# A column per chunk for the output scales, k's features one slot behind q's, and v's parts counted against their due slot

## The chip, the core and the metric

The kernel runs on one NeuronCore of a Trainium2 chip. Five engines work side by side, each on its own queue of instructions in a fixed order: TensorE (PE in the profile, its weight loads PEld), VectorE (DVE), ScalarE (ACT), GpSimd (POOL) and SyncE (SP), which here only starts DMAs. An engine whose next instruction has to wait stands, with everything queued behind it. The metric is the device time of one execution in microseconds.

## The reference

Random-feature attention for 8 batches, 8 heads, 576 positions, 64 dimensions and 128 features, and a bilinear feed-forward block behind it:

```python
q_s, k_s = (q * scale, k * scale)
def phi(x):
    proj = np.einsum('bhsd,md->bhsm', x, omega)
    sq = np.sum(x * x, axis=-1, keepdims=True) / 2.0
    h = proj - sq
    h = h - np.max(h, axis=-1, keepdims=True)
    return np.exp(h) / np.sqrt(m)
q_p, k_p = (phi(q_s), phi(k_s))
kv = np.einsum('bhsm,bhsd->bhmd', k_p, v)
z = np.sum(k_p, axis=2)
num = np.einsum('bhsm,bhmd->bhsd', q_p, kv)
den = np.einsum('bhsm,bhm->bhs', q_p, z)[..., None] + 1e-06
x = num / den                       # to 4608 tokens x 512
out = ((x @ w1) * (x @ w2)) @ w3 @ w_out
```

The kernel subtracts no square: it falls away with the maximum that is subtracted behind it. It multiplies w3 and w_out into one matrix first.

## The kernel before

The 4608 positions are 36 chunks of 128. A batch is 576 positions, so it covers four and a half chunks, and its sum over k needs five of them. Every float32 operand of a matmul is split into two float16 parts, `hi` and `lo`, after a scaling by a power of two, and each product is three matmuls (`PASSES`). The split is the helper at L137: ACT writes `hi`, DVE subtracts to get `lo` (L144; qhl, khl, vhl, xhl in the profile).

A chunk of q or k goes through these stages. `load` (L211) brings it into one of two raw buffers. `norm` (L223) takes its square sum on ACT (L158, junk_q and junk_k) and `scale` (L229) turns this into a scale by way of a small matmul (norm_q_k). `split_raw` (L238) splits it, after which the chunk two further on is loaded. `features` (L250) projects it on PE into two PSUM banks (L265, qpj and kpj), takes the maximum on DVE (L275, nm), subtracts it (L288, qe and ke) and takes the exponential on ACT (L289). `in_parts` (L292) splits the features: for q DVE casts (L130, eq) and POOL subtracts (L298); for k ACT casts (L132, ek) and POOL subtracts.

q's features are turned by a DMA and multiplied by a batch's key-value sum in `q_attend` (L370; PE's nu at L381, then gd, gr and xs on DVE, then mx, the maximum over xs). `kv_batch` (L339) makes that sum (PE's kvp at L346, kv on ACT and DVE). The projections, nu and kvp all take their PSUM from one pool of two buffers (`banks`, L110): each waits until the reader of the buffer two before it is through, which is qe, ke, xs or kv. `x_turn` (L406) scales and splits the attention's output (xhl), turns it by a DMA into xT, and keeps the power of two in pt.

The feed-forward block works on pairs of chunks: `gate` (L604; PE's ab at L617, asb on ACT at L626 and on DVE at L627, then two POOL instructions into the arena) and `project_out` (L637; osc at L639, PE's o at L643, ACT's scaled copy o at L647, and the DMA to the output). osc is one column, pt times pt times the weights' scale kap, out of four rotating buffers (`small`, L116): a new one waits until the ACT copy that read the buffer's last content is done.

v goes through a list of parts per batch (`v_batch`): five square sums on ACT, a scale, five splits. `v_unit` takes one part from the list's head.

What is written when is set by a table of slots. A step i begins at slot `begin[i]`, three slots a step, and treats q's chunk i and k's chunk i + 5. In every slot one unit is taken from the queue of gates and output projections, then the functions that were put at the slot run in the order of their rank, then one part of v's list runs. A scheduler that keeps the program's data dependencies lays the instructions into the engines' queues; it moves an instruction ahead of others where it takes its operands to be ready. So osc, which the program writes with its output projection, stands on DVE several slots ahead of it.

Of the kernel before, what the change touches and what calls it, by code (L numbers as in the profile page):

```python
# [9 lines left out]
F32 = mybir.dt.float32  # L10
# [9 lines left out]
P = 128  # L20
# [30 lines left out]
EAGER = 40  # L51
EARLY = 6
KV_LAG = 5
RAW64_BUFS = 3
O_BUFS = 2
RAW_BUFS = 2
# [10 lines left out]
def tile_favor_attention_then_bilinear_ffn(  # L67
# [20 lines left out]
    NCH = qT.shape[0]  # L88
# [14 lines left out]
    const = ctx.enter_context(tc.tile_pool(name="const", bufs=1))  # L103
# [9 lines left out]
    def bank_m(name):  # L113
        return ps_m.tile([P, 512], F32, tag="pm", name=name)

    def small(name, n=1, rows=P, dt=F32, bufs=4):  # L116
        return sm.tile([rows, n], dt, tag=f"s_{name}", name=name, bufs=bufs)
# [16 lines left out]
    def pick(kinds, i):  # L134
        return kinds[min(i, len(kinds) - 1)]
# [68 lines left out]
    def chunks_of(b):  # L204

        lo, hi = b * S, (b + 1) * S
        return [(c, max(lo - c * P, 0), min(hi - c * P, P)) for c in range(lo // P, -(-hi // P))]
# [10 lines left out]
    for i in range(4):  # L218
        t = const.tile([P, 3], F32, name=f"sums_{i}")
# [3 lines left out]
    def norm(keys, n):  # L223
        am = sums[n % len(sums)]
        for i, k in enumerate(keys):
            square_sum(am[:, i : i + 1], raws[k], f"{k[0]}{k[1]}", QK_PRE)
        return am
# [10 lines left out]
    def split_raw(c, name):  # L238

        raw = raws.pop((name, c))  # L240
        s, es = scales.pop((name, c))
        hl = at.tile([P, 2, NP, P], F16, tag="hl", name=f"{name}hl_{c}", bufs=2)
        split(pick(KS if name == "k" else QS, c), hl[:, 0], hl[:, 1], raw, s)
        hls[name, c] = hl, es
# [5 lines left out]
    def features(c, name):  # L250


        hl, es = hls.pop((name, c))
        pg = banks(f"{name}pj_{c}").rearrange("p g (i m) -> p g i m", m=M)
        pj = pg.rearrange("p g i m -> p (g i) m")

        def project(first=None):
            for i in range(NP):
                if first is not None:
                    for g in range(2):  # L260
                        nc.tensor.matmul(pg[:, g, i], ident, first(g * NP + i), start=True, stop=False)
                for n, (x, y) in enumerate(PASSES):
                    for g in range(2):
                        d = slice(g * D, (g + 1) * D)
                        nc.tensor.matmul(  # L265
                            pg[:, g, i],
                            hl[d, x, i],
                            om[d, y],
                            start=first is None and n == 0,
                            stop=n == len(PASSES) - 1,  # L270
                        )

        project()
        nm = small("nm", H)
        nc.vector.tensor_reduce(nm, pj, AX.X, ALU.max, negate=True)  # L275
        e = at.tile([P, H, M], F32, tag="e", name=f"{name}e_{c}", bufs=2)
        kind = pick(DK if name == "k" else DQ, c)
        if kind == "2":

            project(lambda h: nm[:, h : h + 1].broadcast_to([P, M]))  # L280
            nc.scalar.activation(e, pj, AF.Exp, scale=es, bias=ln_e)
        elif kind == "1":

            nc.vector.tensor_scalar(nm, nm, es, 15 * math.log(2.0), ALU.mult, ALU.add)
            for h in range(H):
                nc.scalar.activation(e[:, h], pj[:, h], AF.Exp, scale=es, bias=nm[:, h : h + 1])
        else:
            nc.vector.tensor_tensor(e, pj, nm.unsqueeze(2).broadcast_to([P, H, M]), ALU.add)  # L288
            nc.scalar.activation(e, e, AF.Exp, scale=es, bias=ln_e)  # L289
        return e  # L290

    def in_parts(t, e, hi, lo):  # L292

        if hi == "p":
            nc.gpsimd.tensor_scalar(t[:, 0], e, 1.0, 1.0, ALU.mult, ALU.mult)
        else:
            copy(hi == "d", t[:, 0], e)
        (nc.vector if lo == "d" else nc.gpsimd).tensor_tensor(t[:, 1], e, t[:, 0], ALU.subtract)  # L298
# [3 lines left out]
    def k_chunk(c):  # L302
        e = features(c, "k")
        ek[c] = at.tile([P, 2, H, M], F16, tag="ek", name=f"ek_{c}", bufs=EK_BUFS)
        in_parts(ek[c], e, pick(EH, c), pick(EL, c))
# [136 lines left out]
    arena = const.tile([P, ARENA, 512], F32, name="arena")  # L442
    raw_at = list(range(0, 4 * RAW64_BUFS, 4))
    mag_at = list(range(4 * RAW64_BUFS, 4 * RAW64_BUFS + 4, 2))
    free = list(range(4 * RAW64_BUFS + 4, ARENA))

# [6 lines left out]
    def used(at):  # L453

        left[at] -= 1
        if not left[at]:
            free.append(at)
# [146 lines left out]
    def gate(c0, n, u):  # L604
# [28 lines left out]
        for k in range(nf):  # L633
            for t in range(n):
                hs[c0 + t, u * nf + k] = h[:, :, k, t * P : (t + 1) * P], place

    def project_out(c):  # L637
        sc = small("osc")
        nc.vector.tensor_scalar(sc, pts[c], pts[c], kap, ALU.mult, ALU.mult)  # L639
        ps = bank_m(f"o_{c}")  # L640
        mm = [(f, a, b) for f in range(NF) for a, b in PASSES]
        for i, (f, a, b) in enumerate(mm):
            nc.tensor.matmul(ps, hs[c, f][0][:, a], W[f][:, b], start=i == 0, stop=i == len(mm) - 1)  # L643
        for f in range(NF):
            used(hs[c, f][1])
        o = mo.tile([P, DO], F32, tag="o", name=f"o_{c}", bufs=O_BUFS)
        nc.scalar.mul(o, ps, sc)  # L647
        nc.sync.dma_start(out[c * P : (c + 1) * P, :], o)
# [3 lines left out]
    B_OF_K = {}  # L652
# [3 lines left out]
    v_work = []  # L656
# [7 lines left out]
    def v_unit():  # L664
        if v_work:
            v_work.pop(0)[1]()
# [26 lines left out]
    for ch in ORDER:  # L693
        n = seen.get(ch, 0)
# [23 lines left out]
    def put(slot, rank, fn):  # L718
        plan.setdefault(slot, []).append((rank, len(plan[slot]) if slot in plan else 0, fn))

    behind_by = []

    def ready(c):
        x_turn(c)
        for c0, m in groups:
            if c0 + m == c + 1:
                units = []
                for u in range(2 * m):
                    need = [(n, u // m) for n in range(2)]
                    units.append((need, lambda c0=c0, m=m, u=u: gate(c0, m, u)))  # L730

                for k, f in enumerate(behind_by):
                    units.insert(2 + 3 * k, f)
                behind_by[:] = [(["k"], lambda c=c: project_out(c)) for c in range(c0, c0 + m)]
                queue.extend(units)
                if c + 1 == NCH:
                    queue.extend(behind_by)

    def step(i):
        at0 = begin[i]  # L740
        kc = i + LEAD
        keys = [(n, c) for n, c in (("q", i), ("k", kc)) if 0 <= c < NCH]
        state = {}

        def norms():
            state["am"] = norm(keys, i)

        def splits():
            for name, c in keys:
                split_raw(c, name)  # L750
                if c + 2 < NCH:
                    load(srcs[name], c + 2, name)

        put(at0 - 3, 3, norms)
        put(at0 - 2, 6, lambda: scale(keys, state["am"]))
        put(at0 - 1, 8, splits)
        if i >= 0:
            put(at0, 1, lambda: q_chunk(i))
            lag = 2 if i < EARLY else 5
            put(at0 + lag, 7 if i < EARLY else 0, lambda: q_attend(i))  # L760
            put(at0 + lag + 1, 0, lambda: ready(i))
        if kc < NCH:
            put(at0, 2, lambda: k_chunk(kc))
        if kc in B_OF_K:

            def kv():

                while v_work and v_work[0][0] <= B_OF_K[kc]:
                    v_unit()
                kv_batch(B_OF_K[kc])  # L770


            put(at0 + (2 if i < 0 else KV_LAG - 1 if i < EARLY else KV_LAG), 5, kv)
        for b in range(B):
            cs = [c for c, _, _ in chunks_of(b)]
            if cs[1] == kc:
                put(at0, 9, lambda b=b: v_batch(b))
            if cs[0] == kc:
                put(at0 + 2, 10, lambda cs=cs: [v_load(c) for c in cs if c not in vraw])
# [7 lines left out]
    for t in range(max(plan) + 1):  # L787
        n = min(PER[t] if t < len(PER) else 1, len(ticks))
        weights(n)
        if not ticks and raw_at:  # L790
            for a, w in [(a, 4) for a in raw_at] + [(a, 2) for a in mag_at]:
                free.extend(range(a, a + w))
            raw_at.clear()
        unit(RESERVE if t > EAGER else 0)
        for _, _, fn in sorted(plan.get(t, []), key=lambda x: x[:2]):
            fn()
        v_unit()
    assert not ticks
    while queue:
        unit()  # L800
# [38 lines left out]
```

## Time and profile before

| | |
|---|---|
| median of 3 runs | 906.85 us (904.66 to 910.05) |
| the profiled execution | 904.25 us |
| its span, from the first to the last instruction | 902.5 us |
| PE busy | 790.9 us (88%) |
| DVE busy | 622.6 us (69%) |
| ACT busy | 421.0 us (47%) |
| POOL busy | 322.2 us (36%) |
| granted TensorE clock, mean | 0.951 |

In a row of groups stand line, engine, operation, what is written and read, shapes and count; then busy time in us and the mean of one in ns; then the engine's idle time just ahead of these instructions and what ended it. In a row of time stand the start, the duration, and in brackets the idle time before it with what ended it; a run of equal instructions is one row. A row of windows has the stretch, its length, the busy time of PE, PEld, DVE, ACT and POOL with the number of instructions, the granted clock, the busy share of the DMA engines and GB/s.

### The profile page before, as it was taken

What the parts mean: (1) busy time and instruction counts of PE and PEld (TensorE: products, weight loads), DVE (VectorE), ACT (ScalarE), POOL (GpSimd) and SP (SyncE); (2) the same over time, 40 slices, a digit from 0 to 9 for tenths busy, and PEclk for the clock granted to TensorE, in tenths of its full rate; (3) what the DMA queues carried; (4) which work ended last, traced back from release to release, by engine and by line L of the source; (5) the groups of instructions that cost most, each with busy time, mean ns of one, the idle gap of its engine ahead of it and who ended that gap; (6) DMA issues with size and microseconds to landing.
All of it is one profiled execution on the core that took longest, in us unless ns stands there. A gap on an engine that the chain in (4) does not pass through costs nothing.

```text
span 902.5 us, 20601 instructions
## 1 busy us (share of the span) xinstructions
PE 790.9 (88%) x8614; PEld 586.0 (65%) x8614; DVE 622.6 (69%) x1116; ACT 421.0 (47%) x748; POOL 322.2 (36%) x327
## 2 busy tenths in 40 slices
PE   1964499578996998999999999899899899999998
PEld 0433254476875876767777776777677677677674
DVE  5879877788779887766867777778667774553210
ACT  3677874877436535444354335543454333221111
POOL 0000003223364465443634643455444543323221
PEclk9985699789999999999999999999999999999999
DMA  8535455332345353333434443344332232333000
GB/s 311 191 120 196 140 153 170 111 73 55 88 107 105 84 130 83 83 84 83 116 83 77 95 111 71 72 94 113 85 93 65 60 71 61 82 60 60 24 25 35
DMA packets 142525, 88.43 MB, mean 98 GB/s; under 512 B 116704, under 2 KB 116832, under 8 KB 142432
## 3 DMA queue, kind: packets, MB, share of 16 engines
q1 hardware_dynamic: 134944, 66.15, 31.0%
q10 hardware_dynamic: 7488, 20.97, 6.9%
q8 instruction: 67, 1.10, 0.5%
q14 instruction: 26, 0.21, 0.1%
HBM read 49.35 MB, written 9.44 MB: 65 GB/s over the span
## 4 chain that ended last, share of the span: by engine, by line
PE 42%; DVE 28%; ACT 13%; DMA 9%; issue 6%; POOL 1%; SPq 0%; DVEq 0%; ACTq 0%; POOLq 0%
PE ab L617 20%; PE o L643 11%; DVE nm L275 5%; DVE qhl L144 4%; DMA qraw<-qT 4%; PE wp L557 4%; DVE vhl L144 3%; ACT ke L289 2%; DVE qe L288 2%; DVE ke L288 2%; DMA kraw<-kT 2%; ACT ek L132 2%; PE kvp L346 2%; DVE asb L627 2%; PE nu L381 1%
## 5 line engine op out<-in xcount | busy, mean ns | idle before, releaser
L617 PE MATMUL ab<-xT,w12b 128*128 128x256 f16 (+1 forms) x3840 | 400.3, 265 | 10.8 <-DMA xT<-xhl 8.5
L617 PEld LDWEIGHTS <-w12b 128*128 128x128 f16 x3840 | 345.1, 99 | 54.3 <-issue 8.8
L643 PE MATMUL o<-Wb,arena 128*128 128x512 f16 x864 | 193.4, 379 | 2.1 <-DVE Wb L144 1.6
L643 PEld LDWEIGHTS <-arena 128*128 128x128 f16 x864 | 84.3, 100 | 96.3 <-issue 2.9
L631 POOL TENSOR_SCALAR arena<-asb 128x512 f16<-128x512 f32 x72 | 57.6, 800 | 249.7 <-DVE asb L627 238.3
L298 POOL TENSOR_TENSOR eq<-qe,eq 128x1024 f16<-128x1024 f32 x34 | 73.9, 2174 | 147.9 <-DVE eq L130 111.1
L289 ACT ACTIVATE qe<-qe,ln_e,es 128x1024 f32<-128x1024 f32 x31 | 38.4, 1239 | 138.0 <-DVE qe L288 138.0
L632 POOL TENSOR_TENSOR arena<-asb,arena 128x512 f16<-128x512 f32 x72 | 91.4, 1270 | 5.9
L627 DVE TENSOR_TENSOR asb<-ab,asb 128x512 f32<-128x512 f32 x72 | 49.4, 686 | 52.7 <-PE ab L617 50.6
L144 DVE SCALAR_TENSOR_TENSOR qhl<-qraw,s,qhl 128x512 f16<-128x512 f32 x36 | 63.8, 1773 | 28.7 <-ACT qhl L141 28.7
L158 ACT ACTIVATE junk_q<-qraw 128x512 bf16<-128x512 f32 x36 | 22.7, 630 | 120.4 <-DMA qraw<-qT 120.3
L298 POOL TENSOR_TENSOR ek<-ke,ek 128x1024 f16<-128x1024 f32 x28 | 60.2, 2149 | 41.4 <-DVE ek L130 39.8
L265 PE MATMUL kpj<-om,khl 64*128 64x128 f16 x864 | 36.9, 237 | 43.4 <-DVE xs L396 12.1
L639 DVE TENSOR_SCALAR osc<-pt,kap 128x1 f32<-128x1 f32 x36 | 9.5, 271 | 84.8 <-ACT o L647 84.6
L265 PEld LDWEIGHTS <-khl 64*128 64x128 f16 x864 | 29.4, 103 | 50.2 <-ACT junk_k L158 16.1
L557 PE MATMUL wp<-w12b 128*128 128x512 f32 x128 | 60.2, 623 | 1.2 <-DVE w12b L485 1.2
L626 ACT ACTIVATE asb<-ab 128x512 f32<-128x512 f32 x72 | 41.8, 580 | 24.4 <-PE ab L617 24.4
L381 PEld LDWEIGHTS <-eqT 128*128 128x128 f16 (+1 forms) x960 | 32.5, 102 | 26.0 <-DMA eqT<-eq 15.3
L647 ACT ACTIVATE o<-o,osc 128x512 f32<-128x512 f32 x36 | 24.2, 673 | 52.2 <-PE o L643 52.2
L381 PE MATMUL nu<-kv,eqT 128*128 128x65 f16 (+1 forms) x960 | 34.7, 196 | 15.0 <-DMA eqT<-eq 14.3
L418 DVE SCALAR_TENSOR_TENSOR xhl<-xs,p2r,xhl 128x512 f16<-128x512 f32 x36 | 28.8, 800 | 26.5 <-ACT xhl L417 26.4
L143 POOL TENSOR_SCALAR vhl<-vraw,s 128x512 f16<-128x512 f32 (+1 forms) x35 | 36.3, 1054 | 29.4 <-DVE mx L409 11.7
(124 smaller groups left out, 1071.1 us busy)
## 6 DMA issues: line engine op xcount, KB each, us to landing
kraw<-kT SPq DMA_DIRECT2D x36, 256.0 KB, 3.0
vraw<-v SPq DMA_DIRECT2D x36, 256.0 KB, 3.0
qraw<-qT SPq DMA_DIRECT2D x36, 256.0 KB, 2.7
out<-o SPq DMA_DIRECT2D x36, 256.0 KB, 2.0
arena<-w3T ACTq DMA_DIRECT2D x8, 1024.0 KB, 5.9
arena<-w ACTq DMA_DIRECT2D x8, 1024.0 KB, 5.6
arena<-wo ACTq DMA_DIRECT2D x4, 1024.0 KB, 5.1
eqT<-eq SPq DMA_TRANSPOSE x72, 3.1
```

Source lines behind the costliest of these rows:

```text
L144: nc.vector.scalar_tensor_tensor(lo, src, s, hi, ALU.mult, ALU.subtract)
L265: nc.tensor.matmul(pg[:, g, i], hl[d, x, i], om[d, y], start=first is None and n == 0, stop=n == len(PASSES) - 1,)
L275: nc.vector.tensor_reduce(nm, pj, AX.X, ALU.max, negate=True)
L289: nc.scalar.activation(e, e, AF.Exp, scale=es, bias=ln_e)
L298: (nc.vector if lo == "d" else nc.gpsimd).tensor_tensor(t[:, 1], e, t[:, 0], ALU.subtract)
L381: nc.tensor.matmul(nu[r0:r1, h // 4, h % 4], t[:, x, place(h), r0:r1], kvs[b][:, y, h], start=n == 0, stop=n == 2,)
L557: nc.tensor.matmul(ps, w[:, j, k * P : (k + 1) * P], guest[:, j], start=j == j0, stop=j == HALF - 1,)
L617: nc.tensor.matmul(ps[:, k], w12[m][i][cc][:, a, r * P : (r + 1) * P], x[:, b, cc, off : off + T], start=j == 0, stop=j == len(mm) - 1,)
L627: nc.vector.tensor_tensor(asb, ab[1], asb, ALU.mult)
L631: nc.gpsimd.tensor_scalar(h[:, 0], asb, 1.0, 1.0, ALU.mult, ALU.mult)
L632: nc.gpsimd.tensor_tensor(h[:, 1], asb, h[:, 0], ALU.subtract)
L643: nc.tensor.matmul(ps, hs[c, f][0][:, a], W[f][:, b], start=i == 0, stop=i == len(mm) - 1)
```

## The change

Three edits. The scales of the outputs get one tile with a column for each of the 36 chunks in the place of four rotating buffers. From step 8 on (`K_LATE`), k's features are put one slot later than q's. And in each slot, as many parts of v are taken as keep every batch's parts in time for its slot `due`, at least one.

```diff
+K_LATE = 8
...
+    oscs = const.tile([P, NCH], F32, name="oscs")
+
     def project_out(c):
-        sc = small("osc")
+        sc = oscs[:, c : c + 1]
         nc.vector.tensor_scalar(sc, pts[c], pts[c], kap, ALU.mult, ALU.mult)
...
+    due = {}
...
         if kc < NCH:
-            put(at0, 2, lambda: k_chunk(kc))
+            put(at0 + (i >= K_LATE), 2, lambda: k_chunk(kc))
...
-            put(at0 + (2 if i < 0 else KV_LAG - 1 if i < EARLY else KV_LAG), 5, kv)
+            due[B_OF_K[kc]] = at0 + (2 if i < 0 else KV_LAG - 1 if i < EARLY else KV_LAG)
+            put(due[B_OF_K[kc]], 5, kv)
...
-        v_unit()
+
+        n = max([1] + [-(-(k + 1) // max(due[b] - t, 1)) for k, (b, _) in enumerate(v_work)])
+        for _ in range(n):
+            v_unit()
```

On PE the kpj groups of the last 21 chunks of k (15 to 35, steps 10 to 30) each stand behind the next gate unit instead of right behind qpj; nothing else moves there. DVE's queue in step 15 (a name's number after the tile is the chunk; the last one is a buffer), before:

```order
L275 TENSOR_REDUCE nm_5588<-qpj_15_5563 128x8
L288 TENSOR_TENSOR qe_15_5590<-qpj_15_5563,nm_5588 128x1024
L275 TENSOR_REDUCE nm_5624<-kpj_20_5599 128x8
L288 TENSOR_TENSOR ke_20_5626<-kpj_20_5599,nm_5624 128x1024
L130 CAST eq_15_5593<-qe_15_5590 128x1024
L627 TENSOR_TENSOR asb_10_3_5688<-ab_10_3_1_5663,asb_10_3_5688 128x512
L173 TENSOR_SCALAR norm_q16_k21_5693<-norm_q16_k21_5693 128x3
```

and with the change, from two instructions earlier:

```order
L643 TENSOR_SCALAR oscs_114<-pt_13_5548,kap_111 128x1
L419 SCALAR_TENSOR_TENSOR xhl_13_5551<-xs_13_5472,p2r1_4_5546,xhl_13_5551 128x512
L628 TENSOR_TENSOR asb_10_2_5538<-ab_10_2_1_5513,asb_10_2_5538 128x512
L276 TENSOR_REDUCE nm_5580<-qpj_15_5555 128x8
L289 TENSOR_TENSOR qe_15_5582<-qpj_15_5555,nm_5580 128x1024
L131 CAST eq_15_5585<-qe_15_5582 128x1024
L628 TENSOR_TENSOR asb_10_3_5647<-ab_10_3_1_5622,asb_10_3_5647 128x512
L276 TENSOR_REDUCE nm_5677<-kpj_20_5652 128x8
L174 TENSOR_SCALAR norm_q16_k21_5685<-norm_q16_k21_5685 128x3
L289 TENSOR_TENSOR ke_20_5679<-kpj_20_5652,nm_5677 128x1024
```

k's maximum and subtraction moved behind q's cast and the second gate's asb. The column of the output scale for chunk 13 now stands right behind its pt, ahead of xhl; before, it stood ahead of the next xs.

ACT's queue from k's exponential on, before:

```order
L289 ACTIVATE ke_19_5318<-ke_19_5318,ln_e_82,es_4979 128x1024
L132 CAST ek_19_5321<-ke_19_5318 128x1024
L141 ACTIVATE qhl_15_5484<-qraw_15_4772,s3_4_5391 128x512
L141 ACTIVATE khl_20_5489<-kraw_20_4777,s3_4_5391 128x512
L158 ACTIVATE junk_q17_5922,sums_1_103<-qraw_17_5487 128x512
L647 ACTIVATE o_8_5424<-o_8_5399,osc_5397 128x512
L158 ACTIVATE junk_k22_5924,sums_1_103<-kraw_22_5492 128x512
L417 ACTIVATE xhl_13_5559<-xs_13_5480,p2r1_4_5554 128x512
```

and with the change:

```order
L290 ACTIVATE ke_19_5374<-ke_19_5374,ln_e_82,es_4973 128x1024
L142 ACTIVATE qhl_15_5476<-qraw_15_4766,s3_4_5384 128x512
L133 CAST ek_19_5377<-ke_19_5374 128x1024
L142 ACTIVATE khl_20_5481<-kraw_20_4771,s3_4_5384 128x512
L651 ACTIVATE o_8_5416<-o_8_5391,oscs_114 128x512
L159 ACTIVATE junk_q17_5880,sums_1_103<-qraw_17_5479 128x512
L418 ACTIVATE xhl_13_5551<-xs_13_5472,p2r1_4_5546 128x512
L627 ACTIVATE asb_10_2_5538<-ab_10_2_0_5488 128x512
L159 ACTIVATE junk_k22_5882,sums_1_103<-kraw_22_5484 128x512
```

k's cast moved behind qhl, and the square sum of the q that is being loaded moved behind the outputs' copy o; k's square sum moved behind xhl and the next asb.

POOL's queue in step 15, before:

```order
L298 TENSOR_TENSOR eq_15_5593<-qe_15_5590,eq_15_5593 128x1024
L298 TENSOR_TENSOR ek_20_5629<-ke_20_5626,ek_20_5629 128x1024
L631 TENSOR_SCALAR arena_112<-asb_10_3_5688 128x512
L632 TENSOR_TENSOR arena_112<-asb_10_3_5688,arena_112 128x512
L143 TENSOR_SCALAR vhl_4_18_5926<-vraw_18_5178,s1_3_5782 128x8x64
```

and with the change:

```order
L299 TENSOR_TENSOR eq_15_5585<-qe_15_5582,eq_15_5585 128x1024
L632 TENSOR_SCALAR arena_112<-asb_10_3_5647 128x512
L633 TENSOR_TENSOR arena_112<-asb_10_3_5647,arena_112 128x512
L299 TENSOR_TENSOR ek_20_5682<-ke_20_5679,ek_20_5682 128x1024
L144 TENSOR_SCALAR vhl_4_18_5884<-vraw_18_5171,s1_3_5773 128x8x64
```

ek's subtraction moved behind the two gate instructions. On SP, the DMA of an output row block moved ahead of k's load; the other transfers keep their order.

## The prediction

> **What bounds the kernel now.** I read the page's shares first, then the busy time of each engine in the stretch that the change touches, then PE's groups of instructions there with the idle time ahead of them.
>
> ```profile
> span 902.5 us, 20601 instructions
> PE 790.9 (88%) x8614; PEld 586.0 (65%) x8614; DVE 622.6 (69%) x1116; ACT 421.0 (47%) x748; POOL 322.2 (36%) x327
> ...
> 310.53:741.99 431.46, 405.85 (x4597) 312.19 (x4596) 317.09 (x546) 190.72 (x310) 207.00 (x191) 0.98 0.37 87
> ...
> L617 PE MATMUL ab<-xT,w12b 128*128 128x256 f16 x1947 | 225.0, 277 | 0.0
> L643 PE MATMUL o<-Wb,arena 128*128 128x512 f16 x480 | 106.8, 379 | 0.2 <-DVE asb L627 0.2
> L265 PE MATMUL kpj<-om,khl 64*128 64x128 f16 x456 | 18.0, 231 | 25.5 <-DVE xs L396 10.9 <-DVE kv L356 9.2 <-ACT junk_k L158 5.3
> ```
>
> The third row is the stretch from q's chunk 10 to q's chunk 31: 21 steps, 20.55 us each. PE is busy 405.85 of its 431.46 us, so it idles 25.6 us. The groups (of 330 to 745 us) show where: 25.5 us ahead of k's projection, 0.2 us ahead of everything else. So PE is the bound except at one instruction, and that one waits for a reader on DVE. One step in order of time shows which:
>
> ```profile
> 436.60 1.21 DVE L275 TENSOR_REDUCE nm<-qpj 128x8 f32<-128x1024 f32 x1
> ...
> 437.84 1.22 DVE L288 TENSOR_TENSOR qe<-qpj,nm 128x1024 f32<-128x1024 f32 x1
> ...
> 439.16 1.24 ACT L289 ACTIVATE qe<-qe,ln_e,es 128x1024 f32<-128x1024 f32 x1 [7.96 <-DVE qe L288]
> 440.23 1.23 DVE L288 TENSOR_TENSOR ke<-kpj,nm 128x1024 f32<-128x1024 f32 x1
> ...
> 441.49 1.24 ACT L289 ACTIVATE ke<-ke,ln_e,es 128x1024 f32<-128x1024 f32 x1 [0.61 <-DVE ke L288]
> ...
> 442.76 0.17 DVE L176 TENSOR_SCALAR norm_q_k<-norm_q_k 128x3 f32<-128x3 f32 x1
> 442.97 0.18 DVE L178 RECIPROCAL s<-norm_q_k 128x3 f32<-128x3 f32 x1
> 443.06 0.19 DVE L232 TENSOR_SCALAR es<-norm_q_k,unom 128x3 f32<-128x3 f32 x1
> ...
> 443.71 0.72 ACT L141 ACTIVATE qhl<-qraw,s 128x512 f16<-128x512 f32 x1
> 444.22 2.13 POOL L298 TENSOR_TENSOR ek<-ke,ek 128x1024 f16<-128x1024 f32 x1
> ...
> 444.46 2.44 DVE L144 SCALAR_TENSOR_TENSOR qhl<-qraw,s,qhl 128x512 f16<-128x512 f32 x1 [1.21 <-ACT qhl L141]
> ...
> 446.82 1.09 DVE L144 SCALAR_TENSOR_TENSOR khl<-kraw,s,khl 128x512 f16<-128x512 f32 x1
> 446.93 0.33 SPq L213 DMA_DIRECT2D qraw<-qT  x1
> ...
> 449.66 0.63 ACT L158 ACTIVATE junk_q<-qraw 128x512 bf16<-128x512 f32 x1 [4.62 <-DMA qraw<-qT]
> ...
> 450.29 0.67 ACT L647 ACTIVATE o<-o,osc 128x512 f32<-128x512 f32 x1
> ...
> 450.99 0.27 DVE L639 TENSOR_SCALAR osc<-pt,kap 128x1 f32<-128x1 f32 x1 [2.76 <-ACT o L647]
> ...
> 451.18 0.68 DVE L396 TENSOR_TENSOR xs<-nu,gr 128x512 f32<-128x512 f32 x1
> ...
> 451.90 0.69 DVE L403 TENSOR_REDUCE mx<-xs 128x1 f32<-128x512 f32 x1
> ...
> 452.01 1.47 PE L265 MATMUL kpj<-om,khl 64*128 64x128 f16 x24 [2.68 <-DVE xs L396]
> ...
> 455.25 0.75 DVE L418 SCALAR_TENSOR_TENSOR xhl<-xs,p2r,xhl 128x512 f16<-128x512 f32 x1 [1.98 <-ACT xhl L417]
> ```
>
> When qhl's split frees the raw buffer (444.46 + 2.44 = 446.90), SP loads the next q; ACT stands at its square sum until the load lands (449.66), then scales the outputs `o`. A one-column DVE instruction, `osc`, wants a buffer of which only four exist and stands 2.76 us until that scaling is done. `xs`, queued behind it, frees the PSUM bank that kpj needs, and PE stands 2.68 us.
>
> Next come DVE's groups of the 21 steps, and what a PE pause costs beyond itself: windows of 3.4 us behind three pauses (busy time of PE, PEld, DVE, ACT and POOL, then the granted clock), and the gate unit behind two of them.
>
> ```profile
> L144 DVE SCALAR_TENSOR_TENSOR qhl<-qraw,s,qhl 128x512 f16<-128x512 f32 x21 | 48.3, 2300 | 23.5 <-ACT qhl L141 23.5
> L627 DVE TENSOR_TENSOR asb<-ab,asb 128x512 f32<-128x512 f32 x43 | 29.4, 684 | 5.1 <-PE ab L617 4.5 <-ACT asb L626 0.6
> ...
> L418 DVE SCALAR_TENSOR_TENSOR xhl<-xs,p2r,xhl 128x512 f16<-128x512 f32 x21 | 17.6, 836 | 16.1 <-ACT xhl L417 16.0
> ...
> L639 DVE TENSOR_SCALAR osc<-pt,kap 128x1 f32<-128x1 f32 x21 | 5.7, 273 | 56.4 <-ACT o L647 56.4
> ...
> 349.01:352.42 3.41, 3.17 (x33) 2.51 (x34) 2.59 (x8) 1.21 (x2) 0.00 (x0) 0.50 0.20 77
> ...
> 721.07:724.48 3.41, 3.41 (x18) 2.43 (x17) 2.70 (x6) 1.20 (x2) 0.85 (x2) 0.50 0.14 29
> 579.40:582.80 3.40, 3.40 (x48) 3.02 (x49) 3.30 (x4) 0.46 (x1) 1.78 (x2) 1.00 0.16 30
> ...
> 349.25 1.46 PE L265 MATMUL kpj<-om,khl 64*128 64x128 f16 x24 [3.80 <-DVE xs L396]
> 350.65 6.26 PE L617 MATMUL ab<-xT,w12b 128*128 128x256 f16 x48
> ...
> 579.40 0.85 PE L265 MATMUL kpj<-om,khl 64*128 64x128 f16 x24 [3.26 <-DVE kv L356]
> 580.18 5.41 PE L617 MATMUL ab<-xT,w12b 128*128 128x256 f16 x48
> ```
>
> DVE idles 431.46 - 317.09 = 114.4 us, half of it (56.4) at osc, and only 4.5 us for PE at asb: in these steps DVE's own sequence of work and waits sets the pace, and PE's pauses are where it shows. After 349.25 the granted clock is 0.50 for 3.41 us: (1.46 - 0.85) + (6.26 - 5.41) = 1.5 us lost on top of 3.80. After 579.40 it is 1.00 and nothing more is lost. The trace has five such half-clock windows from 345 us on (the first at 349.01, the last at 721.07), so 5 x 1.5 = 7.5 us. [...]
>
> **The change part by part.** *The column per chunk.* osc no longer reuses a buffer, so what remains is its wait for pt, which DVE has just made. Removed from DVE: 56.4 us in the 21 steps (2.69 each). The waits outside these steps lie at the end, where no k is projected and nothing stops PE; I count nothing there. The instruction itself (0.27 us) moves between pt and xhl, into the wait that xhl has anyway.
>
> *k's features a slot later.* No instruction is added; kpj stands behind the next gate unit on PE, 5.41 us later. For PE that is cover: the bank's reader (xs, or kv in the steps with a key-value sum) may be 5.41 us later before PE stands, and the longest pause is 3.80. All 25.5 us could go, with the 7.5 us behind them. What stands nearer now is the key-value sum, which takes the bank that ke frees; a whole output projection and nu still lie between.
>
> On DVE the move has a price, since q's cast no longer has k's reduction and subtraction ahead of it while ACT takes the exponential. The trace has this very order at the end, where no k is left; xhl's usual wait stands there too:
>
> ```profile
> 745.84 0.69 DVE L130 CAST eq<-qe 128x1024 f16<-128x1024 f32 x1 [1.31 <-ACT qe L289]
> ...
> 748.42 0.87 DVE L144 SCALAR_TENSOR_TENSOR qhl<-qraw,s,qhl 128x512 f16<-128x512 f32 x1 [0.68 <-ACT qhl L141]
> ...
> 758.08 0.75 DVE L418 SCALAR_TENSOR_TENSOR xhl<-xs,p2r,xhl 128x512 f16<-128x512 f32 x1 [0.73 <-ACT xhl L417]
> ```
>
> So 21 x 1.31 = 27.5 us added at the cast. Queued behind it are asb, k's maximum and ke, all of which PE waits for only by way of banks. The second price is at qhl: cast and asb used to lie between ke and qhl; now three small operations do (0.17 + 0.18 + 0.19 = 0.54), while ACT needs ke's exponential and qhl's scaling in a row: 441.49 + 1.24 + 0.72 - (440.23 + 1.23) = 1.99 us after ke ends. The wait becomes 1.99 - 0.54 = 1.45 against 23.5 / 21 = 1.12: 21 x 0.33 = 6.9 us. The bounds of these two: nothing if DVE is late at another place anyway, 2 us a step if ACT is busy when it is asked.
>
> On ACT the scaling of o now stands ahead of the square sum that waits for q's load, and xhl's scaling ahead of v's square sums. In the four steps with those sums xhl waits about 1.98 instead of 0.73: 4 x 1.25 = 5 us back.
>
> *v's parts.* A queue of 11 parts is opened at a step's start and its sum is due 11 slots later for the first batch, 13 or 14 for the others; the new count is ceil(11 / 11) = 1 or ceil(11 / 14) = 1, and stays 1 as both shrink together. By the table of slots every part is issued where it was. Cost and gain nothing; the longer queue that would need two in a slot does not occur.
>
> *The sum.* DVE: -56.4 + 27.5 + 6.9 - 5.0 = -27.0 us. PE could give 25.6 + 7.5 = 33.1, so DVE still sets the pace, though only by 6 us in 431. Two engines that close stop each other in turn: DVE waits for PE in a step with a key-value sum and PE for DVE in one with v's splits. Today DVE's wait for PE at asb is 4.5 us; I take 5 more, and get -22 us. The profiled execution is 904.25 us (its span 902.5 and 1.75 around it), so 882; the median shown is 2.6 above that execution, and I put the changed kernel at 884.
>
> **The rivals.** *PE alone is the bound.* With ek's subtraction on POOL now behind ke's cast, and qhl's scaling ahead of that cast on ACT, qhl's split on DVE can be through before POOL begins: 0.87 us (748.42, no ek there) instead of 2.44. khl's then takes the meeting, from 1.09 to at most some 2.2. That is 0.5 us a step or 10 us, DVE falls below PE, and the whole 33 goes: 871 by the profiled execution, 874 by the median. For it: qhl and xhl have one form, and 2300 against 836 ns. [...]
>
> *The wait moves to xhl.* ACT's square sum of q still waits for its load, and xhl's scaling now stands right behind it. If 1.05 of the 2.69 us come back there, the prices of 1.31 + 0.33 eat the rest: 902 to 908. The race is close: the load lands 449.66 - 446.90 = 2.8 us after qhl's split and o starts 0.6 later (450.29), 3.4 in all, while on DVE khl, xs and mx take 1.09 + 0.68 + 0.69 = 2.5 us and six operations as small as the three above come between them and p2r, another 1.0: even, so little of the wait should come back.
>
> *Slower.* ACT stands twice in DVE's sequence, at the cast and at qhl. If the exponential of q is found behind k's square sum, which waits for k's load, or behind three of v's, 2 us more at the cast give 1.31 + 0.33 + 2.0 - 2.69 = +0.95 a step, 20 us: 924. From 1.05 us on it decides. Against it: in the step above ACT had stood idle 7.96 us when qe came.
>
> **How the numbers follow.** My forecast 0.62 (876 to 896), PE alone 0.19 (871 to 876), the wait moved 0.12, slower 0.07. About 0.5%, 4.5 us, is what a measurement can tell. Faster is the first two and a sixth of the third, 0.83; the same 0.10; slower 0.07. The range leaves out the last two: 871 to 900.
>
> **What would show it.** Osc's group with no idle from ACT; kpj's idle in the stretch under 5 us instead of 25.5; eq's cast with 1.3 us of idle each, up to 28 in all; no or one half-clock window behind kpj; 19.4 to 19.6 us a step. Wrong it is if xhl's wait for ACT grows well over 16 us, if the cast waits over 2 us a time, or if PE's idle appears at kvp or qpj instead.

## The result and the profile after

The changed kernel takes 876.88 us (median of 4 runs, 875.45 to 879.70) beside 907.68 us (now also 4 runs, 904.66 to 910.05) before: a ratio of 0.967, 95% interval 0.963 to 0.971. Its profiled execution took 877.26 us, 27.0 less than that of before. Forecast was 884, with 871 to 900 as the range.

The page's shares of the changed kernel, then the windows view of the 21 steps in both kernels, this time cut at PE's own instructions, from q's projection of chunk 10 to that of chunk 31 (columns as before: stretch, its length, PE, PEld, DVE, ACT, POOL, granted clock).

```profile
span 875.4 us, 20594 instructions
PE 788.7 (90%) x8608; PEld 583.0 (67%) x8614; DVE 612.7 (70%) x1116; ACT 417.2 (48%) x748; POOL 307.3 (35%) x327
```

```profile
309.93:712.23 402.30, 402.30 (x4613) 307.13 (x4613) 306.31 (x544) 185.94 (x308) 192.42 (x191) 1.00 0.40 94
```

```profile
307.92:739.25 431.33, 405.72 (x4614) 312.14 (x4614) 316.51 (x542) 191.38 (x312) 207.00 (x191) 0.98 0.37 87
```

The stretch became 431.33 - 402.30 = 29.0 us shorter; 2.0 of this are lost ahead of it (it begins at 309.93 instead of 307.92), and behind it nothing moved (163.2 us in both): 27.1 us of span. In the changed kernel PE is busy in all of it (402.30 us), at full clock (1.00; 0.98 before). PE's groups from 330 to 715 us say the same, with nothing left ahead of kpj:

```profile
L618 PE MATMUL ab<-xT,w12b 128*128 128x256 f16 x1935 | 218.2, 273 | 0.0
...
L266 PE MATMUL kpj<-om,khl 64*128 64x128 f16 x480 | 16.9, 217 | 0.0
```

DVE's groups (310.82 to 714.32 us, the 21 steps as the prediction cut them) show where its waits went:

```profile
L145 DVE SCALAR_TENSOR_TENSOR khl<-kraw,s,khl 128x512 f16<-128x512 f32 x20 | 42.0, 2098 | 16.1 <-ACT khl L142 16.1
L628 DVE TENSOR_TENSOR asb<-ab,asb 128x512 f32<-128x512 f32 x42 | 28.7, 684 | 4.3 <-PE ab L618 3.8 <-ACT asb L627 0.5
...
L419 DVE SCALAR_TENSOR_TENSOR xhl<-xs,p2r,xhl 128x512 f16<-128x512 f32 x21 | 17.6, 837 | 6.5 <-ACT xhl L418 6.1
L145 DVE SCALAR_TENSOR_TENSOR qhl<-qraw,s,qhl 128x512 f16<-128x512 f32 x21 | 15.8, 752 | 32.3 <-ACT qhl L142 32.3
L131 DVE CAST eq<-qe 128x1024 f16<-128x1024 f32 x21 | 14.6, 694 | 27.8 <-ACT qe L290 27.8
...
L643 DVE TENSOR_SCALAR oscs<-pt,kap 128x1 f32<-128x1 f32 x21 | 5.7, 269 | 0.6
```

osc's 56.4 us are gone, xhl's 16.1 became 6.5, and the cast waits 27.8, qhl 32.3 (23.5 before) and khl 16.1 (nothing before). qhl's split is down from 2300 to 752 ns and khl's up from 1091 to 2098. The timeline of one step shows why:

```profile
436.45 1.23 DVE L289 TENSOR_TENSOR ke<-kpj,nm 128x1024 f32<-128x1024 f32 x1
...
437.77 1.24 ACT L290 ACTIVATE ke<-ke,ln_e,es 128x1024 f32<-128x1024 f32 x1 [3.33 <-DVE norm_q_k L177]
...
438.92 0.70 ACT L142 ACTIVATE qhl<-qraw,s 128x512 f16<-128x512 f32 x1
439.53 1.03 ACT L133 CAST ek<-ke 128x1024 f16<-128x1024 f32 x1
439.65 0.75 DVE L145 SCALAR_TENSOR_TENSOR qhl<-qraw,s,qhl 128x512 f16<-128x512 f32 x1 [1.58 <-ACT qhl L142]
440.43 0.33 SPq L214 DMA_DIRECT2D qraw<-qT  x1
...
440.63 2.13 POOL L299 TENSOR_TENSOR ek<-ke,ek 128x1024 f16<-128x1024 f32 x1 [1.92 <-ACT ek L133]
441.09 0.67 ACT L651 ACTIVATE o<-o,oscs 128x512 f32<-128x512 f32 x1
441.21 2.09 DVE L145 SCALAR_TENSOR_TENSOR khl<-kraw,s,khl 128x512 f16<-128x512 f32 x1 [0.81 <-ACT khl L142]
...
443.09 0.63 ACT L159 ACTIVATE junk_q<-qraw 128x512 bf16<-128x512 f32 x1 [1.34 <-DMA qraw<-qT]
```

qhl's split ends (440.40) before POOL begins ek's subtraction (440.63), and takes 0.75 us; khl's runs beside that subtraction from 441.21 to 442.76 and takes 2.09. In the kernel before, qhl's ran beside it and took 2.44, and khl's came behind it and took 1.09. Why a split takes longer beside it is not shown. khl has first waited 0.81 us, since ek's cast stands ahead of its scaling on ACT. The outputs' scaling (441.09) is through before ACT stands at the load.

### The profile page after: what moved, and what is told of

It is laid out like the page before. It is cut to its first block, busy times and chain, and to the rows that moved or that the text cites. A ratio compares the mean times of both kernels' runs of the same rounds, so it can differ in the third digit from the quotient of the medians.

```text
span 875.4 us, 20594 instructions
## 1 busy us (share of the span) xinstructions
PE 788.7 (90%) x8608; PEld 583.0 (67%) x8614; DVE 612.7 (70%) x1116; ACT 417.2 (48%) x748; POOL 307.3 (35%) x327
## 3 DMA queue, kind: packets, MB, share of 16 engines
q1 hardware_dynamic: 134944, 66.15, 32.3%
## 4 chain that ended last, share of the span: by engine, by line
PE 76%; DVE 10%; ACT 6%; DMA 4%; issue 3%; POOL 1%; SPq 0%; ACTq 0%; DVEq 0%; POOLq 0%
PE ab L618 40%; PE o L647 21%; PE wp L558 4%; PE nu L382 3%; PE qpj L266 3%; PE kvp L347 3%; PE kpj L266 2%; DVE vhl L145 1%; ACT qe L287 1%; DVE nm L276 1%; ACT ke L287 1%; DVE arena L485 1%; DMA arena<-wo 1%; PE norm_q_k L164 1%; DVE w12b L486 1%
## 5 line engine op out<-in xcount | busy, mean ns | idle before, releaser
L618 PE MATMUL ab<-xT,w12b 128*128 128x256 f16 (+1 forms) x3840 | 395.3, 264 | 8.6 <-DMA xT<-xhl 6.2
L632 POOL TENSOR_SCALAR arena<-asb 128x512 f16<-128x512 f32 x72 | 48.4, 672 | 217.8 <-DVE asb L628 205.9
L633 POOL TENSOR_TENSOR arena<-asb,arena 128x512 f16<-128x512 f32 x72 | 84.7, 1177 | 6.0
L290 ACT ACTIVATE ke<-ke,ln_e,es 128x1024 f32<-128x1024 f32 x27 | 33.5, 1241 | 78.6 <-DVE ke L289 62.0
L145 DVE SCALAR_TENSOR_TENSOR khl<-kraw,s,khl 128x512 f16<-128x512 f32 x36 | 55.4, 1540 | 16.2 <-ACT khl L142 16.1
L145 DVE SCALAR_TENSOR_TENSOR qhl<-qraw,s,qhl 128x512 f16<-128x512 f32 x36 | 32.3, 898 | 38.1 <-ACT qhl L142 38.1
L651 ACT ACTIVATE o<-o,oscs 128x512 f32<-128x512 f32 x36 | 24.2, 673 | 53.5 <-PE o L647 53.5
L418 ACT ACTIVATE xhl<-xs,p2r 128x512 f16<-128x512 f32 x36 | 25.8, 718 | 45.4 <-DVE p2r L188 44.4
L558 PEld LDWEIGHTS wp<-w12b 128*128 128x128 f32 x128 | 25.0, 199 | 32.3 <-issue 29.2
```

Of the source, the lines that this page charges most:

```text
L145: nc.vector.scalar_tensor_tensor(lo, src, s, hi, ALU.mult, ALU.subtract)
L558: nc.tensor.matmul(ps, w[:, j, k * P : (k + 1) * P], guest[:, j], start=j == j0, stop=j == HALF - 1,)
L618: nc.tensor.matmul(ps[:, k], w12[m][i][cc][:, a, r * P : (r + 1) * P], x[:, b, cc, off : off + T], start=j == 0, stop=j == len(mm) - 1,)
L632: nc.gpsimd.tensor_scalar(h[:, 0], asb, 1.0, 1.0, ALU.mult, ALU.mult)
L633: nc.gpsimd.tensor_tensor(h[:, 1], asb, h[:, 0], ALU.subtract)
```

## The experiments

Ratios are to the kernel before on the same chip: 905.10 us there for the first four runs, 905.89 for the next four, 907.25 and 903.46 for the two runs with third buffers, 907.05 for the last two.

**One part alone, and the changed kernel again.** `column_only` has the column and nothing else; `kslot_only` has the slot of k and nothing else. v's parts alone were not run: built, they leave every engine's queue as it was.

```diff
# column_only
+    oscs = const.tile([P, NCH], F32, name="oscs")
-        sc = small("osc")
+        sc = oscs[:, c : c + 1]
# kslot_only
+K_LATE = 8
-            put(at0, 2, lambda: k_chunk(kc))
+            put(at0 + (i >= K_LATE), 2, lambda: k_chunk(kc))
```

> Only the column per chunk; k's features stay behind q's, v as before. My account (the column takes osc's wait off xs, the k slot covers what is left): osc's idle 0 instead of 56.4 us; xs is no longer behind it, so the kpj pauses behind xs go, while those behind kv stay in part because ACT still scales xhl behind q's and k's square sums, which wait for loads; DVE's pace 19.2 to 19.6 us a step, 880 to 890 us. Rival: the column is the whole change, 875 to 879 us, no PE idle left. Rival: the wait comes back at xhl and the k slot is the whole change, over 898 us.

> Only k's features a slot later; osc keeps its four buffers. In its order ACT scales o ahead of the square sum that waits for q's load, which is what osc had waited for. My account: osc's idle falls under 0.5 us a step, by that order and not by the column, and 877 to 882 us follow. Rival: the buffer is the matter, osc keeps some 2.5 us a step, the cast's 1.3 us come on top, and the time is 900 us or more.

> The changed kernel itself beside the others on one chip, as the measure for what is built on it: 875 to 880 us, 0.963 to 0.971 of the kernel before.

| | us | ratio, 95% interval |
|---|---|---|
| column alone | 887.07 | 0.981 (0.978 to 0.984) |
| k's slot alone | 875.33 | 0.968 (0.966 to 0.971) |
| the whole change again | 877.24 | 0.969 (0.968 to 0.971) |

PE's and DVE's groups with the column alone, over the same 21 steps (311.92 to 723.16 us):

```profile
L265 PE MATMUL kpj<-om,khl 64*128 64x128 f16 x504 | 18.8, 225 | 10.0 <-DVE kv L356 9.7 <-DVE xs L396 0.2
```

```profile
L418 DVE SCALAR_TENSOR_TENSOR xhl<-xs,p2r,xhl 128x512 f16<-128x512 f32 x21 | 17.0, 808 | 42.3 <-ACT xhl L417 41.9
```

Without its buffer osc waits no more, but 26 of the 56 us come back at xhl, which stands behind the same square sums on ACT; four pauses ahead of kpj stay. With k's slot alone osc still has four buffers, and yet (DVE's groups, 308.49 to 711.97 us):

```profile
L640 DVE TENSOR_SCALAR osc<-pt,kap 128x1 f32<-128x1 f32 x21 | 5.5, 261 | 0.8 <-ACT o L648 0.8
```

The slot of k alone brings o ahead of q's square sum on ACT, and with that the whole gain. The column adds nothing that can be measured.

**Where k's slot begins.** The new pause early in the run (2.80 us ahead of kvp at 299.41) lies in steps 8 and 9.

```diff
-K_LATE = 8
+K_LATE = 10
```

> The change with K_LATE = 10 instead of 8. In the changed kernel PE pauses 2.80 us at kvp behind ke at 299 us and loses some 1.7 us to a half clock behind it; chunks 13 and 14 of k are the two that are put late there without a gate to cover them. My account: this pause goes, 3 to 4.5 us less than the changed kernel (872 to 874). Rival: the pause moves to another bank or to xT, no difference (876 to 878).

Measured 877.29 us, 0.970 (0.967 to 0.972): no difference. The pause at kvp went, and one of 2.06 us ahead of ab, for xT's transfer, came in its place at 302.67.

**The root, by leaving the loads out.** In the kernel before, q's loads from chunk 10 on and k's from chunk 15 on are left out, and the chunk two before is used again. Nothing else changes: kpj still right behind qpj, four buffers for osc.

```diff
+                raw = raws[name, c]
-                if c + 2 < NCH:
+                if i >= 8 and c + 2 < NCH:
+                    raws[name, c + 2] = raw
+                elif c + 2 < NCH:
                     load(srcs[name], c + 2, name)
```

> The kernel before without the loads of q from chunk 10 and of k from chunk 15 on: the two tiles of each that are there are used again, so these loads are left out and the outputs are of other data; nothing else is changed, k's features stand right behind q's, osc has four buffers. It asks whether the root was ACT's wait for those loads. Account A (the load that ACT waits for in front of o and xhl is the root): osc's idle falls under 10 us of 56, kpj's pauses under 5 us, 875 to 882 us. Account B (kpj needs the gate as cover whatever ACT does): the pauses behind kv stay, 884 to 892 us.

Measured 869.26 us, 0.961 (0.959 to 0.963), below even account A's range. The windows row, again from PE's projection of chunk 10 to that of chunk 31:

```profile
308.07:704.02 395.95, 395.95 (x4613) 307.27 (x4613) 299.72 (x545) 189.76 (x306) 207.43 (x191) 1.00 0.31 69
```

PE is busy throughout without any cover for kpj: what was late was ACT, standing at its loads. (That freer DMA queues helped, 69 GB/s beside 87, this run alone does not exclude; the last two runs do, with all loads made.) And the same 4613 matmuls take 395.95 us, 6.35 less than in the changed kernel, where PE does not stand either; the last section comes back to this.

**Which engine is the bound now.** Two more matmuls of 512 columns per output projection (some 15.6 us of PE), and one more maximum over xs per step from chunk 10 on (26 of 0.69 us, 17.9 us of DVE), both in the changed kernel; what they write is overwritten. A third run takes k's slot alone and keeps one unit of gates and projections in reserve instead of two.

```diff
# pe_more, in project_out
+        for _ in range(2):
+            nc.tensor.matmul(ps, hs[c, 0][0][:, 0], W[0][:, 0], start=True, stop=True)
# dve_more, in q_attend
-        nc.vector.tensor_reduce(mx, xs, AX.X, ALU.max, apply_absolute_value=True)
+        for _ in range(1 + (c >= 10)):
+            nc.vector.tensor_reduce(mx, xs, AX.X, ALU.max, apply_absolute_value=True)
# kslot_reserve1
-RESERVE = 2
+RESERVE = 1
```

> The changed kernel with two matmuls of 512 columns more in each of the 36 output projections (the first product is made again and overwritten): 72 x 0.22 = 15.6 us of PE. If PE alone is the bound from the first projection on, 13 to 16 us more than the changed kernel (890 to 893). If DVE sets the pace in the steps with k, only the 15 projections before and after them count: 5 to 8 us more.

> The changed kernel with the maximum over xs taken twice on DVE from chunk 10 on: 0.69 us more in each of 26 steps, 21 of them with k. If DVE is at its limit in those: 12 to 15 us more. If PE is the bound and DVE has more than a percent or two to spare: 0 to 1 us. My account, from the sum (DVE's pace and PE's within 1%, DVE some 5 us behind before a bank is missed): 3 to 9 us more.

> k's features a slot later alone, with one unit of the gates' queue held back in place of two. In the changed kernel PE still pauses 4.9, 1.5 and 2.8 us between 276 and 300 us, where the queue is being filled, and runs some us at half clock there. If this reserve is only a buffer: 3 to 8 us less than the k slot alone (868 to 873). If two units are needed, xT is missed later on and the time is 876 us or more.

Measured 891.66 us (0.985, 0.983 to 0.987), 882.83 (0.976, 0.973 to 0.978) and 889.65 (0.983, 0.981 to 0.984). Against the changed kernel's 877.24 in the runs before these, PE's 15.6 us cost 14.4, and DVE's 17.9 cost 5.6. Of DVE's 17.9, 13.0 lie in the 21 steps and make them 6.2 us longer (402.30 before); the rest lies behind them and costs nothing. So PE is the bound, and DVE is some 7 us behind it. The 21 steps with DVE longer:

```profile
309.11:717.62 408.51, 403.45 (x4613) 307.65 (x4612) 315.53 (x559) 186.09 (x308) 191.72 (x191) 1.00 0.40 91
```

PE's pauses show there at the key-value sum (PE's groups, 310 to 725 us). One unit in reserve missed its forecast of 868 to 873, and its pauses show at q's projection (310 to 730 us):

```profile
L347 PE MATMUL kvp<-vhl,ek 128*128 128x65 f16 x480 | 15.2, 193 | 4.1 <-DVE ke L289 4.1
```

```profile
L266 PE MATMUL qpj<-om,qhl 64*128 64x128 f16 x504 | 18.6, 217 | 6.0 <-DVE qhl L145 6.0
```

In the changed kernel DVE takes 17.6 us from one maximum of q to the next in a step without splits of v and about 23 in one with all of them, and PE 18.4 in a plain step: with two units in reserve PE passes the long ones without a pause, with one it stands 7.7 us in the 21 steps.

**Curing the root without moving k.** Two runs give raw buffers a third place, so that a load is issued a step earlier: for q alone (taking one of the key-value sums' three buffers), and for q and k (taking one of xT's three). Both have the column and keep kpj behind qpj.

```diff
# third_q_buffer; third_buffers has 3 for both and xT with 2
-        t = at.tile(..., name=f"{name}raw_{c}", bufs=RAW_BUFS)
+        t = at.tile(..., name=f"{name}raw_{c}", bufs=RAW_BUFS + (name == "q"))
...
         def norms():
             state["am"] = norm(keys, i)
+            for name, c in keys:
+                if c + 2 < NCH and name == "q":
+                    load(srcs[name], c + 2, name)
```

> The kernel before, with kpj still right behind qpj, and the column for the outputs' scale, but with a third raw buffer for q whose load is issued a step earlier; its space comes from the key-value sums, which get two buffers instead of three. Account A (the root is ACT standing at a load that it reaches too early; k's features need no other slot): k's raw buffer is free at 446.82 + 1.09 = 447.91 in the step that the prediction showed, its load lands some 2.8 us later at 450.7 and its square sum is through at 451.3, before xhl's scaling is wanted (about 452.5). Then kpj stands under 5 us in all from 310 us on, PE keeps the cheaper order in which kpj follows qpj (396.0 us in the 21 steps when no load was waited for, against 403.5 with k's features a slot later), and the time is 867 to 873, below the changed kernel. Account B (a wait for k's load is as bad, since it stands ahead of xhl as in the run with the column alone): xhl waits 1.5 us or more a step, kpj's pauses stay in the steps with a key-value sum, and the time is 880 to 890. Two buffers for the key-value sums cost nothing as long as nu of the batch two before is through; if not, kv on ACT and DVE stands for PE's nu, and the time is above 890.

> The kernel before, with kpj still right behind qpj, and the column for the outputs' scale, but with a third raw buffer for q and for k, and both loads issued a step earlier; the space comes from xT, which gets two buffers instead of three. Account A (ACT standing at loads that it reaches too early is the root, and one of the two loads is enough to bring the wait to xhl, as in the run with the third buffer for q alone): junk_q and junk_k wait for no load any more, xhl's wait for ACT falls to 1 us or less a step, kpj's pauses go, and the time is 867 to 875. Account B (the pauses come from pairing kpj with qpj itself, and leaving out the loads helped only because the DMA queues were freer): the pauses ahead of kpj in the four steps with a key-value sum stay at 1.8 us or more, 880 to 890. If two buffers of xT are too few, xT's transposes stand on SP for PE's gates with the loads behind them, and the time is above 890.

Measured 901.85 us (0.993, 0.991 to 0.996) and 882.52 (0.976, 0.974 to 0.979). My account missed both times. ACT's groups, of the first and of the second kernel (310 to 730 us), and the second one's rows on DVE and PE:

```profile
L158 ACT ACTIVATE junk_k<-kraw 128x512 bf16<-128x512 f32 x19 | 12.0, 630 | 82.1 <-DMA kraw<-kT 82.1
```

```profile
L158 ACT ACTIVATE junk_q<-qraw 128x512 bf16<-128x512 f32 x21 | 13.2, 630 | 95.4 <-DMA qraw<-qT 95.4
```

```profile
L418 DVE SCALAR_TENSOR_TENSOR xhl<-xs,p2r,xhl 128x512 f16<-128x512 f32 x22 | 18.0, 818 | 40.6 <-ACT xhl L417 40.5
```

```profile
L265 PE MATMUL kpj<-om,khl 64*128 64x128 f16 x504 | 17.6, 216 | 6.1 <-DVE kv L356 5.7 <-DVE xs L396 0.4
```

With the third buffer for q alone, ACT stood at k's load. With both, the loads went out a step earlier and the scheduler moved the square sums a step earlier too: in ACT's built queue they stand right behind their loads again, with o and xhl behind them. The time of the second, 882.52, is in account B's range, but not by its mechanism: the last two runs keep kpj behind qpj and have no pause. So it is the place in the queue that has to change, not the load. Their cost beside this (a buffer fewer elsewhere) was not told apart.

**The square sums behind xhl.** The last two runs give q's and k's square sums an operand that exists only once xhl is split: a bias of zeros, made from xhl by one small DVE instruction a step. kpj stays behind qpj. The first has the column, the second keeps osc's four buffers.

```diff
+            nc.scalar.activation(dst, src, AF.Square, scale=pre, bias=zero[-1], accum_out=out)
...
         nc.vector.scalar_tensor_tensor(t[:, 1], xs, r, t[:, 0], ALU.mult, ALU.subtract)
+        zero.append(small("zero", bufs=2))
+        nc.vector.tensor_scalar_mul(zero[-1], t[:, 1, 0:1], 0.0)
```

> The kernel before, with kpj still right behind qpj, and the column for the outputs' scale; the square sums of q and k take as their bias a column of zeros that DVE makes from xhl's split (one DVE instruction of some 0.15 us a step), so on ACT they now stand behind the scaling of o and of xhl in every step, a whole pass of the raw buffers after their loads were issued. Nothing else moves by intent, and no buffer is added. Account A (the root is ACT standing at loads that it reaches too early, with o and xhl queued behind): junk_q and junk_k wait for no load, osc and xhl for ACT 1 us or less a step, kpj's pauses go, PE keeps the cheaper order, and the 21 steps take 396 to 399 us: 868 to 874, below the changed kernel. Account B (with kpj right behind qpj the readers of PSUM are late at a key-value sum whatever ACT does): four pauses of 1.8 us or more ahead of kpj stay, 880 to 890. A new wait is possible at norm_q_k, which now has some 3 us after its square sums; if they are late, qhl and then qpj stand, and the time is above 880.

> As squares_late, but the outputs' scale keeps its four rotating buffers. Account A: with the square sums out of the way, ACT scales o in time and osc waits under 1 us a step; the time is that of squares_late within 3 us. Rival (the four buffers cost by themselves): osc waits 1 us or more a step, xs behind it is late, and the time is 5 us or more above squares_late.

Measured 872.33 us (871.83 to 873.13; 0.963, 0.959 to 0.967) and 871.98 (0.962, 0.959 to 0.966). The first one's windows row of the 21 steps, and its groups on PE, DVE and ACT (310 to 715 us):

```profile
310.84:706.81 395.97, 395.97 (x4613) 307.22 (x4613) 326.11 (x568) 201.30 (x321) 207.51 (x191) 1.00 0.43 95
```

```profile
L270 PE MATMUL kpj<-om,khl 64*128 64x128 f16 x504 | 17.5, 216 | 0.0
...
L423 DVE SCALAR_TENSOR_TENSOR xhl<-xs,p2r,xhl 128x512 f16<-128x512 f32 x21 | 17.6, 837 | 5.6 <-ACT xhl L422 5.3
...
L161 ACT ACTIVATE junk_q<-qraw,zero 128x512 bf16<-128x512 f32 x22 | 15.9, 722 | 24.1 <-DVE zero L425 23.1 <-DMA out<-o 1.0
```

The account held: no wait for a load, no pause, and the 395.97 us of PE that leaving the loads out had given (395.95), now with all loads made. Of the kernels that load all of q and k these two are the fastest here, with k's features where they were; the column makes no difference between them. They ran on another chip than the changed kernel: by the ratios to before the lead is 0.4 to 0.7% (the intervals of the two groups touch), and by the profiled stretch 6.3 us.

## Why the prediction was right, and where not

Right were the direction and the cause: ACT's wait for q's load, by way of o, osc and xs, made kpj late, and 29 us of PE's stretch came back. The cover that k's slot gives kpj left no pause, as said, but it is not what is needed: with ACT's order mended, kpj stands right behind qpj without one.

*The column per chunk.* That osc's 56.4 us would go was right, but I gave the credit to the wrong edit. k's slot alone takes them away, by ACT's new order; the column alone moves 26 of them to xhl. That is the second rival's mechanism, which came true only where k's slot was missing.

*k's slot.* The cast's 27.5 was 27.8, and qhl's 1.45 us a step was 1.54 (8.8 us in all instead of 6.9). xhl gave back 9.6 instead of 5.0. Not foreseen: khl's wait of 0.81 (16.1 us), and on the other side qhl's and khl's splits, together 12.3 us shorter. The first rival had named this exchange (0.87 and at most 2.2 us; 0.75 and 2.10 came), but not the wait; its 2.2 was my estimate. DVE's listed waits and these two splits change by -56.4 + 27.8 + 8.8 + 16.1 - 9.6 - 12.3 = -25.6 us, where the forecast had -27.0.

*v's parts.* Nothing, as said.

*What PE could give.* I had 25.6 + 7.5 = 33.1. The pauses cost more beyond themselves: the stretch's matmuls took 405.72 us, and 395.97 in the same order without a pause, so 9.8. Step by step, the five steps with a half-clock window have 8.4 of this (1.5 to 1.8 each), and eight others with a pause some 0.17 each, where I had counted nothing. And a cost was missing: with k's projection away from q's, they take 402.30, or 6.3 more. So 25.6 + 9.8 - 6.3 = 29.1, less the 2.0 ahead of step 10: the 27.1 measured.

*The sum: the step that failed.* "DVE still sets the pace", and with it "I take 5 more". PE sets it, with no idle at all, and adding work to either engine showed which. The waits that I added up for DVE were real, but DVE's steps are unequal (17.6 and 23 us), and two reserve units even them out; the 5 us of mutual stops came to nothing. With one unit in reserve PE does stand in these steps (7.7 us), and the time is 14 us above k's slot alone. So the first rival was the case: 877 by the profiled execution instead of its 871, for the 6.3 us that no one had counted and the 2.0 ahead of step 10, less the 2.3 that the pauses were worth more. That -27.0 for DVE equals the measured -27.0 is chance: the time was set by PE.

*What would show it.* osc without idle, kpj without idle, the cast at 1.3 us: all seen. 19.4 to 19.6 us a step: 402.30 / 21 = 19.2. Of the things that were to prove it wrong, a pause at kvp did appear, but once, at 299.41, ahead of the steps counted.

## What to carry to other kernels

A wait on the slowest engine is followed back to the instruction that stands at the head of some queue before its data can be there. Its place in the queue is what to mend. Issuing the load earlier did not mend it here: in one run (901.85 us) the wait moved to the next load, in the other (882.52) the scheduler moved the reader up with the load. A cheap operand that exists late enough did (872.33). And when two engines come out as close as here, 6 us in 431 by my sum, lengthen each by a known amount and see how much of it arrives: here a sum of waits had named the wrong one as the bound.

## What was not expected of the hardware

**The same matmuls take longer in another order.** One plain step on PE, of the kernel with the late square sums and of the changed kernel:

```profile
517.98 0.84 PE L270 MATMUL qpj<-om,qhl 64*128 64x128 f16 x24
518.66 0.83 PE L270 MATMUL kpj<-om,khl 64*128 64x128 f16 x24
519.43 5.41 PE L624 MATMUL ab<-xT,w12b 128*128 128x256 f16 x48
524.68 0.28 PE L168 MATMUL norm_q_k<-sums,ones 128*128 128x3 f32 x2
524.82 5.34 PE L652 MATMUL o<-Wb,arena 128*128 128x512 f16 x24
...
536.07 0.84 PE L270 MATMUL qpj<-om,qhl 64*128 64x128 f16 x24
```

```profile
520.39 0.84 PE L266 MATMUL qpj<-om,qhl 64*128 64x128 f16 x24
521.16 5.41 PE L618 MATMUL ab<-xT,w12b 128*128 128x256 f16 x48
526.51 0.84 PE L266 MATMUL kpj<-om,khl 64*128 64x128 f16 x24
527.28 0.38 PE L164 MATMUL norm_q_k<-sums,ones 128*128 128x3 f32 x2
527.53 5.34 PE L647 MATMUL o<-Wb,arena 128*128 128x512 f16 x24
...
538.78 0.84 PE L266 MATMUL qpj<-om,qhl 64*128 64x128 f16 x24
```

18.09 and 18.39 us with the same work. qpj takes 0.68 us from its start to the next one's where kpj follows it, and 0.77 where ab does; ab takes 5.25 ahead of norm_q_k and 5.35 ahead of kpj; norm_q_k 0.14 behind ab and 0.25 behind kpj. 0.09 + 0.10 + 0.11 = 0.30, and 21 x 0.30 = 6.3. Why this order costs more is open.

**The half clock depends on where a pause falls.** In the traces of the kernel before and of the changed one, all half-clock windows of one trace start on one grid of 3.41 us (12 stretches of them in the first, 8 in the second); two of those of the changed kernel start at 275.91 and 299.81, seven windows apart. The clearest case is the pause ahead of kvp in two executions of the changed kernel, 2.80 us in `after` and 2.82 in `after_again`. Cut along the grid, it lies within one window in the first and is split over two in the second:

```profile
296.40:299.81 3.41, 0.61 (x20) 0.49 (x17) 2.34 (x3) 3.41 (x8) 0.00 (x0) 1.00 0.11 22
299.81:303.22 3.41, 3.41 (x68) 3.41 (x65) 2.80 (x12) 3.27 (x4) 3.10 (x3) 0.50 0.73 137
```

```profile
297.95:301.36 3.41, 1.60 (x53) 1.60 (x54) 3.41 (x10) 3.38 (x6) 0.97 (x1) 1.00 0.41 77
301.36:304.77 3.41, 3.41 (x87) 3.27 (x83) 2.80 (x7) 2.70 (x4) 3.33 (x4) 1.00 1.09 112
```

PE idles 2.80 us of the first window, and half clock follows; kvp takes 5.35 us, and step 10 begins at 309.93. In the second execution it idles 1.81 us of the window, and full clock follows; kvp takes 3.80 us, and step 10 begins at 308.74. So the 2.0 us that seemed lost ahead of step 10 are in part luck of the phase. The same cut agrees with the kernel before, where the prediction's steps show half clock behind a pause of 3.80 us (349.25) and full clock behind one of 3.26 (579.40). The second is split into 1.56 and 1.70, and full clock (1.00) follows:

```profile
574.29:577.70 3.41, 1.85 (x34) 1.38 (x32) 2.32 (x8) 3.08 (x7) 0.00 (x0) 1.00 0.20 77
577.70:581.11 3.41, 1.71 (x33) 1.54 (x34) 3.27 (x5) 0.00 (x0) 1.09 (x2) 1.00 0.43 82
581.11:584.52 3.41, 3.41 (x34) 3.06 (x32) 3.31 (x3) 1.72 (x2) 0.69 (x1) 1.00 0.00 0
```

From 220 us to the last outputs, the line lies near 1.85 us of 3.41 in the windows that were cut. In the kernel before, half clock followed the six with 1.95 us idle (492.37) or more, and none with 1.70 (577.70) or less; in the changed kernel it followed 3.41 (272.50) and 2.80 (296.40). 1.85 us brought it in the kernel with one unit in reserve (451.70) and did not in the one with more work on DVE (298.29). With the column alone 2.10 brought it (386.75) and 1.81 did not (666.65). But idle time alone does not set it. In the changed kernel the half clock of 275.91 goes on for a second window although PE idles only 1.08 us of the first; and earlier, where output projections come one or two at a time, 1.42 us idle was enough:

```profile
214.47:217.89 3.42, 2.00 (x12) 0.65 (x11) 3.14 (x7) 1.27 (x2) 0.00 (x0) 1.00 0.00 0
217.89:221.30 3.41, 3.38 (x32) 1.25 (x31) 2.82 (x6) 2.56 (x4) 0.00 (x0) 0.50 0.07 8
```

A matmul of these that stands alone (215.07) counts as busy for 0.38 us, while 24 in a row (527.53) take 5.34; whether that is the reason is open. Either way, the pause of 2.8 us ahead of kvp cost extra in one execution and not in the other, by its phase: 5.35 and 3.80 us for the same kvp.
